# An FFT convolution with an MLP behind it: loads of the first pairs re-ordered, fronts one block earlier, operands moved

## The chip, the cores and the metric

The kernel runs on one core of one Trainium2 chip. Its engines are TensorE (PE, with its weight loads shown apart as PEld), VectorE (DVE), ScalarE (ACT), GpSimd (POOL) and SyncE (SP), which here does nothing but issue DMAs. The metric is device time in microseconds (us) of one execution; the lower the better.

## The reference

Two batches of 12480 positions and 128 channels are convolved along the positions with a long filter, which a small MLP makes from pos_emb; the result is multiplied by x, and its 24960 rows go through a second MLP (128 to 2048 to 128) with a leaky ReLU.

```python
B, S, D = x.shape                                  # 2, 12480, 128
h_mlp = np.maximum(pos_emb @ w1, 0.0) @ w2
h_filt = h_mlp * np.exp(-0.01 * pos)[:, None]
u = x * v
y = irfft(rfft(u, 2 * S) * rfft(h_filt, 2 * S), 2 * S)[:, :S, :]
h = (x * y).reshape(B * S, D) @ w_in               # w_in 128 x 2048
out = np.maximum(0.01 * h, h) @ w_out              # w_out 2048 x 128
```

## The kernel before

The transforms are written as matrix products of lengths 98 (NA) and 128 (NB). **Stage a** (to about 200 us) transforms batch 0 and the filter along 98. **Stage b** (about 200 to 352 us) goes through 25 chunks of 4 frequency rows, in the order ORD: it makes the filter's spectrum (hp, from es, copied by ScalarE at L710; the result hs is also stored to hspec by DMAs that ScalarE issues at L759), transforms the other axis, multiplies, transforms back into dp, copies dp to ct (back_evac, L205) and stores ct in the scratch array scr2. For the first tile of the next stage the last two chunks don't go through scr2: last_c (L588) moves four rows straight from ct into the tile's buffer cin. The preparation of the MLP's weights runs between the chunks.

**The main loop** takes the rest. Its input is cut into 64 tiles t of 390 rows, 32 (NT) for each batch. For each tile:
- load_tile issues 13 DMAs on SP: load_gx the factors gt (L545) and the rows of x called xm (L551, L553, L556), load_c the transform's rows cin (L576, L579, L582). cin has two buffers, as have gt and xm.
- join (join_hi, join_lo) forms sums and differences of cin: two into cp (L600), two into cq (L609), four more into cp (L611). They run on POOL, for tile 0 on VectorE (join_lo alone). cp has one buffer.
- front, first half: 16 matmuls yp (L822) and the product zt (L825, VectorE). Second half, three blocks later: four transposes zp (L830), three copies zf (L833, L835, ScalarE), the rounded part zh (L841, ScalarE) and the remainder zl (L842, POOL).

The MLP works on pieces k of up to 512 columns; a piece takes up one or two tiles. For each of 16 blocks f of the hidden layer m1 issues three matmuls (L849, L850, L851: zh and zl against the high and low parts of the weights), ScalarE and VectorE apply the activation into rh and rl, and three blocks later m2 adds three more matmuls into acc (L881, L882, L883). So a block is six matmuls on PE. When a piece is complete, finish copies its columns out (ot, L896), and at block 4 of the next piece, for a second tile at block 8, transposes them (op, L905, copied by ScalarE to os, L907) and stores them. yp, zp and op are allocated under one PSUM tag, io, with one buffer. The convolution of batch 1 (conv) is fed in between the blocks until about 1090 us.

Everything around the blocks is placed by a table of slots i = 16 k + f. ends[t] is the slot of the second half of front(t): three slots before the piece that first reads the tile, and at least 8 before the next tile's. The first half stands at ends[t] - 3, the join at ends[t] - 11, the loads at ends[t - 2] + 1.

```python
e = min(e - 8, first[t] * NF - 3)
ends[t] = e
...
at(ends[t] - (11 if t % NT > 1 else 8), "join", t)
at(ends[t] - 3, "front", t)
at(ends[t], "front", t)
```

The matmuls of the MLP's m1 and m2 read their moving operands zh, zl, rh and rl from SBUF; in the built program these tiles start 32 bytes past a multiple of 64. Those of the conv (th, tl, ph, pl, L137) start at a multiple of 64.

Of the kernel before, what the change touches and what calls it, by code (L numbers as in the profile page):

```python
# [8 lines left out]
F32 = mybir.dt.float32  # L9
# [21 lines left out]
def tile_conv_mlp(ctx, tc, x, v, pos_emb, w1, w2, w_in, w_out, cf, cr, cg, cb, ci, cw, out):  # L31
    nc = tc.nc
    B, S, D = x.shape
    FO = pos_emb.shape[1]
    DFF = w_in.shape[1]
    NF = DFF // 128
    ROWS = S // NB
    NCH = (NA + KC - 1) // KC
    R0 = 96
    L, H = slice(0, HB), slice(HB, 2 * HB)  # L40
    MID = KH // KC
    ORD = [*range(MID + 1, NCH), MID, *range(MID)]
# [9 lines left out]
    scr2 = [dram.tile([NA, 2 * HB * 256 + 1088], F32, name=f"scr2_{b}")[:, :2 * HB * 256].rearrange(  # L52
        "k (r m e) -> k r m e", r=2, m=HB) for b in range(B)]
# [56 lines left out]
    def run(g):  # L110
        for _ in g:
            pass
# [86 lines left out]
        eng.dma_start(out=scr2[b][k0:k0 + n].rearrange("k r m e -> (r m) k e"),  # L199
                          in_=ct[:, :n].rearrange("p k s d -> p k (s d)"))  # L200

    def back_evac(dp, ct, n):

        for s in range(2):
            nc.scalar.copy(ct[:, :n, s, :], dp[s][:, :n * D].rearrange("p (k d) -> p k d", d=D))  # L205
            yield


    with tc.manual_schedule():
# [3 lines left out]
        def fetch_a(c):  # L213
            ft = s0.tile([128, MC1 * 4 * NA], F32, tag="s0", name="ft1", bufs=3)[:NA].rearrange(
                "a (m p e) -> a m p e", m=MC1, p=2)
            nc.sync.dma_start(out=ft, in_=cf[:, c * MC1:(c + 1) * MC1])
            xv = []
            for i, src in enumerate((x, v)):
                t = s0.tile([128, 1024], F32, tag=f"s{1 + i}", name="xv1", bufs=3 - i)[:NA, :2 * MC1 * D].rearrange(
                    "a (p m d) -> a p m d", p=2, d=D)  # L220
                load_tokens(t, src[1], c * MC1, MC1)
                xv.append(t)
            got[c] = ft, xv
# [312 lines left out]
        xring = Ring("xm", [128, 2, 2, D], slice(32, 64), slice(96, 128))  # L536
        gring = Ring("gt", [128, 4 * NA + 32], (slice(None), slice(4 * NA, None)))
        NT = HB // 2
        ld, z, acc = {}, {}, {}

        def load_gx(t):
            b, mp = divmod(t, NT)
            g = gring()
            for r in range(2):
                nc.sync.dma_start(out=g[KH * r:KH * r + KH, :4 * NA],  # L545
                                  in_=cg[:KH, mp, r].rearrange("k p m a -> k (p m a)"))
            xt = xring()
            ms = slice(2 * mp, 2 * mp + 2)
            full = x[b, :(NA - 2) * NB, :].rearrange("(i w p n) d -> w i p n d", w=2, p=2, n=HB)
            for w in range(2):  # L550
                nc.sync.dma_start(out=xt[64 * w:64 * w + KH - 1], in_=full[w, :, :, ms, :])  # L551
            r0 = (NA - 2) * NB
            nc.sync.dma_start(out=xt[KH - 1:KH],  # L553
                              in_=x[b, r0:r0 + NB, :].rearrange("(o p n) d -> o p n d", o=1, p=2)[:, :, ms, :])
            r0 += NB + 2 * mp
            nc.sync.dma_start(out=xt[GAP - 1:GAP, 0], in_=x[b, None, r0:r0 + 2, :])  # L556
            ld[t] = (None, g, xt)

        def load_c(t):
            b, mp = divmod(t, NT)  # L560
            ci_t = mlp.tile([NA, 3, 2, 2, D], F32, tag="cin", name="cin")
            ld[t] = (ci_t, *ld[t][1:])
            rows_c(t, 1, 0, KH)
            if t:
                rows_c(t, 0, 0, KH)
            else:
                rows_c(t, 0, MID * KC, KH)

        def rows_c(t, j, lo, hi):

            b, mp = divmod(t, NT)
            ci_t = ld[t][0]
            ms = slice(2 * mp, 2 * mp + 2)
            ks = slice(KH * j + lo, KH * j + hi)
            for r in range(2):
                nc.sync.dma_start(out=ci_t[KH * r + lo:KH * r + hi, j].rearrange("k m s d -> k (m s d)"),  # L576
                                  in_=scr2[b][ks, r, ms, :].rearrange("k m e -> k (m e)"))
            if j:
                nc.sync.dma_start(out=ci_t[KH + lo:KH + hi, 2].rearrange("k m s d -> k (m s d)"),  # L579
                                  in_=scr2[b][ks, 0, ms, :].rearrange("k m e -> k (m e)"))  # L580
                for i in range(2):
                    nc.sync.dma_start(out=ci_t[lo:hi, 2, :, i, :], in_=scr2[b][ks, 1, ms, D - D * i:2 * D - D * i])  # L582

        def last_c(ct, k0, n):

            for r in range(2):
                for m in range(2):
                    nc.sync.dma_start(out=ld[0][0][KH * r + k0:KH * r + k0 + n, 0, m],  # L588
                                      in_=ct[HB * r + m:HB * r + m + 1, :n])

        def load_tile(t):
            load_gx(t)
            load_c(t)

        def join_hi(t):

            ci_t, g, xt = ld[t]
            cp = mlp.tile([NA, 2, 2, 2, D], F32, tag="cp", name="cp", bufs=1)
            for p, op in ((0, ALU.add), (1, ALU.subtract)):
                nc.gpsimd.tensor_tensor(out=cp[:, p, 1], in0=ci_t[:, 1 + p, :, 0, :], in1=ci_t[:, 1 + p, :, 1, :], op=op)  # L600
            ld[t] = ci_t, g, xt, cp

        def join_lo(t):
# [10 lines left out]
        with ExitStack() as st:  # L614
# [81 lines left out]
            def ahead(n):  # L696
                for _ in range(4 * n):
                    next(conv)
# [13 lines left out]
            def evac(c):  # L712
                ct = sbb.tile([128, KC, 2, D], F32, tag="ct", name="ct", bufs=2)
                k0, n = chunk(c)
                run(back_evac(dps.pop(c), ct, n))
                if c in ORD[-2:]:
                    last_c(ct, k0, n)
                store_back(0, c, ct, nc.scalar)

            eh, dps = {}, {}  # L720
            ahead(A0)
            next(conv)
            hidden(ORD[0])
            for i, c in enumerate(ORD):
                if i + 2 < NCH:
                    load_b(ORD[i + 2])
                if i == NCH - 9:
                    load_gx(0)
                    load_c(0)
                if i == NCH - 5:  # L730
                    join_hi(0)
                if i == NCH - 3:
                    load_gx(1)
                if i == NCH - 1:
                    rows_c(0, 0, 0, (MID - 2) * KC)
                if i in FETCH:
                    fetch_a(1 + FETCH.index(i))
                if i == NCH - 2:
# [4 lines left out]
                n = chunk(c)[1]  # L743
# [40 lines left out]
            load_c(1)  # L784
            mult_a(2)
            ahead(A2)
            fetch_a(3)
            run(wprep)
            ahead(A3)

# [25 lines left out]
        def front(t):  # L816
# [3 lines left out]
            for q in range(4):  # L820
                for w in range(2):
                    nc.tensor.matmul(yp[64 * w:64 * w + 64, q, :], g[:NA, NA * q + w:NA * q + w + 127:2],  # L822
                                     cp[:, q // 2, w, q % 2, :], start=True, stop=True)
            zt = sm.tile([128, 4, D], F32, tag="zt", name="zt", bufs=1)
            nc.vector.tensor_tensor(out=zt[:GAP], in0=yp[:GAP], in1=xt[:GAP].rearrange("a p m d -> a (p m) d"),  # L825
                                    op=ALU.mult)
            yield
# [90 lines left out]
        first = [next(pieces_of(t))[0] for t in range(total)]  # L918
        ends, e = {}, NTL * NF
        for t in reversed(range(1, total)):  # L920
            e = min(e - 8, first[t] * NF - 3)
            ends[t] = e
        steps = {}

# [140 lines left out]
```

## Time and profile before

| what | value |
|---|---|
| runs | 1757.57 us median of 3 (1754.39 to 1758.05) |
| profiled execution | 1754.5 us |
| its span | 1752.7 us |
| busy, PE | 1666.5 us (95% of the span) |
| busy, DVE | 1112.9 us (63%) |
| busy, ACT | 984.4 us (56%) |
| busy, POOL | 828.7 us (47%) |
| mean granted TensorE clock | 0.977 |

The span is the time between the first and the last instruction of the profiled execution; the execution's own time holds 1.8 us more. A granted clock of 1.00 is TensorE's upper level (2.4 GHz), 0.50 its lower (1.2 GHz); a stretch's value in between is a mean over both. Matmuls overlap: their durations are longer than the distance of their starts, so what one costs in a stream is read from the starts.

### The profile page before, as it was taken

The numbers are of one execution on the slowest core, as the hardware profiler recorded it, in microseconds if no ns is written. First come the engines' busy times: TensorE is split into PE (matmuls) and PEld (weight loads), VectorE is DVE, ScalarE is ACT, GpSimd is POOL, SyncE is SP. The second block draws the span as 40 slices with busy tenths as digits, with TensorE's granted clock in tenths as the row PEclk, the third lists the DMA queues.
The fourth block names the chain that finished last, engine by engine and source line by source line (L and its number), as shares of the span: only waits on it lengthen the run. The fifth ranks groups of instructions, "written<-read, shape, count | busy, mean of one in ns | idle before, by whom it ended". The sixth has DMA issues, their size and how long they took to land. (4 is left out here: it accounts for less than half of the span.)

```text
span 1752.7 us, 27421 instructions
## 1 busy us (share of the span) xinstructions
PE 1666.5 (95%) x9185; PEld 1331.7 (76%) x9185; DVE 1112.9 (63%) x1702; ACT 984.4 (56%) x2006; POOL 828.7 (47%) x860
## 2 busy tenths in 40 slices
PE   6787899869999999999999999999999999999998
PEld 6687455468888878777877787877777777887778
DVE  4576688735545565555655554477777777777775
ACT  2222354424444466666767665566666666666666
POOL 3453121234434367777767674443544454345330
PEclk9889999979999999999999999999999999999999
DMA  9898999864667475656656551312212121212110
GB/s 234 240 269 243 296 324 321 283 180 142 182 172 195 117 197 164 176 149 175 167 144 181 159 153 49 96 49 64 70 49 77 42 73 53 66 46 71 58 32 19
DMA packets 166680, 253.27 MB, mean 145 GB/s; under 512 B 14623, under 2 KB 119347, under 8 KB 163467
## 3 DMA queue, kind: packets, MB, share of 16 engines
q1 hardware_dynamic: 146394, 225.82, 45.2%
q10 hardware_dynamic: 20144, 25.69, 4.3%
q8 instruction: 73, 1.20, 0.3%
q14 instruction: 69, 0.56, 0.1%
HBM read 167.95 MB, written 83.43 MB: 143 GB/s over the span
## 5 line engine op out<-in xcount | busy, mean ns | idle before, releaser
L856 DVE SCALAR_TENSOR_TENSOR rl<-mh,rh 128x512 fp32r<-128x512 f32 (+2 forms) x400 | 269.3, 676 | 315.9 <-ACT rh L855 312.9
L866 DVE TENSOR_TENSOR rl<-r,rh 128x512 fp32r<-128x512 f32 (+1 forms) x400 | 326.2, 828 | 124.6 <-ACT rh L865 117.5
L855 ACT ACTIVATE rh<-mh 128x512 fp32r<-128x512 f32 (+2 forms) x400 | 234.6, 589 | 216.6 <-PE mh L851 199.7
L861 ACT ACTIVATE r<-mh 128x512 f32<-128x512 f32 (+1 forms) x400 | 235.0, 588 | 178.1 <-PE mh L851 165.2
L849 PE MATMUL mh<-zh,w_in_h 128*128 128x512 f32 (+3 forms) x800 | 330.4, 413 | 2.1 <-ACT zh L841 1.3
L850 PE MATMUL mh<-zl,w_in_h 128*128 128x512 f32 (+3 forms) x800 | 313.7, 392 | 6.4 <-POOL zl L842 6.2
L851 PE MATMUL mh<-zh,w_in_l 128*128 128x512 f32 (+3 forms) x800 | 312.6, 391 | 0.0
L883 PE MATMUL acc<-rh,w_out_l 128*128 128x512 f32 (+3 forms) x800 | 312.3, 390 | 0.0
L881 PE MATMUL acc<-rh,w_out_h 128*128 128x512 f32 (+3 forms) x800 | 312.1, 390 | 0.0
L882 PE MATMUL acc<-rl,w_out_h 128*128 128x512 f32 (+3 forms) x800 | 312.1, 390 | 0.0
L611 POOL TENSOR_TENSOR cp<-cq,cp 98x256 f32<-98x256 f32 x252 | 218.6, 867 | 19.8
L842 POOL TENSOR_TENSOR zl<-zf,zh 128x390 fp32r<-128x390 f32 (+24 forms) x110 | 72.3, 670 | 317.1 <-ACT zh L841 194.0
L600 POOL TENSOR_TENSOR cp<-cin 98x256 f32<-98x256 f32 x128 | 103.4, 828 | 202.7 <-PE yp L822 122.9
L849 PEld LDWEIGHTS mh<-zh,w_in_h 128*128 128x128 f32 x800 | 151.1, 189 | 37.6 <-issue 7.6
L850 PEld LDWEIGHTS mh<-zl,w_in_h 128*128 128x128 f32 x800 | 151.7, 190 | 34.9 <-POOL zl L842 10.0
L882 PEld LDWEIGHTS acc<-rl,w_out_h 128*128 128x128 f32 x800 | 150.8, 188 | 34.0 <-DVE rl L866 0.6
L881 PEld LDWEIGHTS acc<-rh,w_out_h 128*128 128x128 f32 x800 | 150.9, 189 | 33.4
L883 PEld LDWEIGHTS acc<-rh,w_out_l 128*128 128x128 f32 x800 | 150.7, 188 | 33.3
L851 PEld LDWEIGHTS mh<-zh,w_in_l 128*128 128x128 f32 x800 | 151.0, 189 | 32.5
L863 DVE CAST rh<-r 128x512 fp32r<-128x512 f32 (+1 forms) x200 | 126.7, 634 | 28.6 <-ACT r L861 25.3
L865 ACT CAST rh<-r 128x512 fp32r<-128x512 f32 (+1 forms) x200 | 121.9, 610 | 6.4
L609 POOL TENSOR_TENSOR cq<-cin 98x256 f32<-98x256 f32 x126 | 104.7, 831 | 2.1 <-DMA cin<-scr 2.1
(152 smaller groups left out, 2369.4 us busy)
## 6 DMA issues: line engine op xcount, KB each, us to landing
cin<-scr SPq DMA_DIRECT2D x318, 98.0 KB
hd<-hspec SPq DMA_DIRECT2D x48, 512.0 KB
scr<-o SPq DMA_DIRECT2D x32, 588.0 KB
bin<-scr SPq DMA_DIRECT2D x23, 768.0 KB
scr1b<-o SPq DMA_DIRECT2D x32, 392.0 KB
hspec<-hs ACTq DMA_DIRECT2D x48, 256.0 KB
scr<-ct ACTq DMA_DIRECT2D x24, 512.0 KB
xm<-in_x_dram SPq DMA_DIRECT2D x128, 96.0 KB
```

Of the source, the lines that this page charges most:

```text
L611: eng.tensor_tensor(out=cp[:, p, w], in0=cq[:, p], in1=cp[:, p, 1], op=op)
L849: nc.tensor.matmul(hp, w_in_h[:, fs], zh, start=True, stop=False)
L850: nc.tensor.matmul(hp, w_in_h[:, fs], zl, start=False, stop=False)
L851: nc.tensor.matmul(hp, w_in_l[:, fs], zh, start=False, stop=True)
L855: nc.scalar.activation(out=rh, in_=hp, func=AF.Relu)
L856: nc.vector.scalar_tensor_tensor(out=rl, in0=hp, scalar=0.0, in1=rh, op0=ALU.max, op1=ALU.subtract)
L861: nc.scalar.activation(out=r, in_=hp, func=AF.Lrelu, alpha=0.01)
L863: nc.vector.tensor_copy(rh, r)
L866: nc.vector.tensor_tensor(out=rl, in0=r, in1=rh, op=ALU.subtract)
L881: nc.tensor.matmul(ap, w_out_h[:, f, :], rh, start=(f == 0 and at0[k] >= S), stop=False)
L882: nc.tensor.matmul(ap, w_out_h[:, f, :], rl, start=False, stop=False)
L883: nc.tensor.matmul(ap, w_out_l[:, f, :], rh, start=False, stop=(f == NF - 1))
```

## The change

The loads of cin's upper halves (one DMA of r = 0, one of r = 1, and so on) become a generator, upper_c, and for tile 0 one of its five steps is taken per chunk from the 16th chunk on, where before all thirteen DMAs of tile 0 stood at the 17th. gt and xm of tile 0 move to the second last chunk, those of tile 1 behind the last rows of tile 0. The two sums of join_hi for tile 0 move from POOL to VectorE, directly ahead of its join_lo. Of the last chunk's four DMAs from ct to cin two are issued by ScalarE, and VectorE makes the second of the two copies to ct. load_tile issues cin ahead of gt and xm. Tile 2 is loaded behind the first half of front(0), and the fetch fetch_a(3) for batch 1, which stood ahead of it, follows. The ends of the fronts are 4 slots ahead of the piece in place of 3; the joins and loads, which count from them, move along. zt is allocated with 856 numbers per partition in place of 512; the tiles behind it, zh, zl, rh and rl among them, then start at a multiple of 64 bytes in the built program, and those of the conv 32 bytes past one.

```diff
-    def back_evac(dp, ct, n):
+    def back_evac(dp, ct, n, other=None):
         for s in range(2):
-            nc.scalar.copy(ct[:, :n, s, :], dp[s][:, :n * D].rearrange("p (k d) -> p k d", d=D))
+            (s and other or nc.scalar.copy)(ct[:, :n, s, :], dp[s][:, :n * D].rearrange("p (k d) -> p k d", d=D))
...
+        def upper_c(t):
+            cin[t] = mlp.tile([NA, 3, 2, 2, D], F32, tag="cin", name="cin")
+            b, ms = t // NT, slice(2 * (t % NT), 2 * (t % NT) + 2)
+            ks = slice(KH, 2 * KH)
+            for r, j in ((0, 1), (1, 1), (0, 2)):
+                p0 = KH * (r if j == 1 else 1)
+                nc.sync.dma_start(out=cin[t][p0:p0 + KH, j].rearrange("k m s d -> k (m s d)"),
+                                  in_=scr2[b][ks, r, ms, :].rearrange("k m e -> k (m e)"))
+                yield
...
-        def last_c(ct, k0, n):
+        def last_c(ct, k0, n, engs):
             for r in range(2):
                 for m in range(2):
-                    nc.sync.dma_start(out=ld[0][0][KH * r + k0:KH * r + k0 + n, 0, m],
+                    engs[m].dma_start(out=cin[0][KH * r + k0:KH * r + k0 + n, 0, m],
                                       in_=ct[HB * r + m:HB * r + m + 1, :n])
         def load_tile(t):
+            load_c(t)
             load_gx(t)
-            load_c(t)
         def join_hi(t):
...
+            eng = nc.gpsimd if t else nc.vector
...
-                if i == NCH - 9:
+                if NCH - 10 <= i < NCH - 5:
+                    next(first_c)
+                if i == NCH - 2:
                     load_gx(0)
-                    load_c(0)
-                if i == NCH - 5:
-                    join_hi(0)
-                if i == NCH - 3:
-                    load_gx(1)
                 if i == NCH - 1:
                     rows_c(0, 0, 0, (MID - 2) * KC)
+                    load_gx(1)
...
-            fetch_a(3)
...
-            zt = sm.tile([128, 4, D], F32, tag="zt", name="zt", bufs=1)
+            zt = sm.tile([128, 856], F32, tag="zt", name="zt", bufs=1)[:, :4 * D].rearrange("a (q d) -> a q d", d=D)
...
-            e = min(e - 8, first[t] * NF - 3)
+            e = min(e - 8, first[t] * NF - 4)
...
         frt = front(0)
+        join_hi(0)
         join_lo(0)
         next(frt)
+        load_tile(2)
+        fetch_a(3)
```

How the change moves rows on the engines is shown at two places. The first is SP's queue between the loads of tile 1 and those of tile 2. In before two fetches for batch 1 (the second ends in the first rows here, L73 and L75) and a store of the conv (L421) stand ahead of tile 2's loads (gt, xm, cin_3247):

```order
L75 DMA xv1_3199<-in_x_dram 1x2x512
L73 DMA xv1_3203<-in_v_dram 96x2x512
L73 DMA xv1_3203<-in_v_dram 1x2x512
L75 DMA xv1_3203<-in_v_dram 1x2x512
L421 DMA scr1b_61<-o1_3106 98x4x256 x2
L545 DMA gt_1329<-in_cg_dram 49x392 x2
L551 DMA xm_1323<-in_x_dram 48x2x256 x2
L553 DMA xm_1323<-in_x_dram 1x2x256
L556 DMA xm_1323<-in_x_dram 1x256
L576 DMA cin_3247<-scr2_0_63 49x512 x2
L579 DMA cin_3247<-scr2_0_63 49x512
L582 DMA cin_3247<-scr2_0_63 49x2x128 x2
```

After the change tile 2's loads (cin_3173, gt, xm) stand directly behind the last loads of tile 1 (cin_3118), and the first fetch (L216, L73) behind them:

```order
L586 DMA cin_3118<-scr2_0_63 49x512 x2
L565 DMA cin_3173<-scr2_0_63 49x512 x3
L569 DMA cin_3173<-scr2_0_63 49x2x128 x2
L586 DMA cin_3173<-scr2_0_63 49x512 x2
L545 DMA gt_1329<-in_cg_dram 49x392 x2
L551 DMA xm_1323<-in_x_dram 48x2x256 x2
L553 DMA xm_1323<-in_x_dram 1x2x256
L556 DMA xm_1323<-in_x_dram 1x256
L216 DMA ft1_3187<-in_cf_dram 98x1568
L73 DMA xv1_3189<-in_x_dram 96x2x512
L73 DMA xv1_3189<-in_x_dram 1x2x512
L75 DMA xv1_3189<-in_x_dram 1x2x512
```

So thirteen loads have moved ahead of two fetches and a store, and cin stands ahead of gt and xm. The second place is PE, in a piece where two tiles become due. In before the transposes op stand at the end of one block and zp at the end of the next; in brackets stands whose semaphore a row waits for:

```order
L905 MATMUL op<-ident,ot 98x128 [waits DVE_49]
L905 MATMUL op<-ident,ot 98x128 [waits Activation_49]
L905 MATMUL op<-ident,ot 98x128 x2
L849 MATMUL mh<-zh,w_in_h 128x512
L850 MATMUL mh<-zl,w_in_h 128x512
L851 MATMUL mh<-zh,w_in_l 128x512
L881 MATMUL acc<-rh,w_out_h 128x512
L882 MATMUL acc<-rl,w_out_h 128x512
L883 MATMUL acc<-rh,w_out_l 128x512
L830 MATMUL zp<-ident,zt 128x113 [waits Activation_49]
L830 MATMUL zp<-ident,zt 128x113 x3
```

After the change, in the same piece (L836 is the line of zp now, L911 that of op, L855 that of the first m1 matmul, L887 to L889 those of m2):

```order
L887 MATMUL acc<-rh,w_out_h 128x512 [waits Activation_49]
L888 MATMUL acc<-rl,w_out_h 128x512
L889 MATMUL acc<-rh,w_out_l 128x512
L836 MATMUL zp<-ident,zt 128x113 [waits DVE_49]
L836 MATMUL zp<-ident,zt 128x113 x3
L911 MATMUL op<-ident,ot 98x128 [waits PE_49,Activation_49]
L911 MATMUL op<-ident,ot 98x128 x3
L855 MATMUL mh<-zh,w_in_h 128x512 [waits DVE_49]
```

zp has moved up by a block and stands directly ahead of op, which takes the same PSUM buffer: op waits for ScalarE, whose last copy out of zp sets it free. PE's rows have zp directly ahead of op 15 times now, nowhere before.

## Rows read from the trace of the kernel before

**Rows 1.** The page's part 1: engine, busy us, share of the span, instructions.

```profile
PE 1666.5 (95%) x9185; PEld 1331.7 (76%) x9185; DVE 1112.9 (63%) x1702; ACT 984.4 (56%) x2006; POOL 828.7 (47%) x860
```

**Rows 2.** Waits of PE up to 390 us: waited for, us in all, times, longest.

```profile
PE hp L749 <- ACT es L710: 10.6, 5, 3.6
...
PE yp L822 <- POOL cp L611: 5.0, 2, 4.6
```

**Rows 3.** Waits of PE from 390 us on.

```profile
PE mh L850 <- POOL zl L842: 6.2, 8, 1.0
PE yp L822 <- POOL cp L611: 2.0, 4, 0.8
```

**Rows 4.** Timeline around the second seam: start, us, engine, line, idle time and releaser.

```profile
369.76 1.98 PE L822 MATMUL yp<-cp,gt 98*64 98x128 f32 x16
...
374.55 0.74 SPq L545 DMA_DIRECT2D gt<-in_cg_dram  x2
...
380.62 0.74 POOL L600 TENSOR_TENSOR cp<-cin 98x256 f32<-98x256 f32 x1 [11.41 <-DMA cin<-scr]
...
383.69 0.72 POOL L600 TENSOR_TENSOR cp<-cin 98x256 f32<-98x256 f32 x1 [2.33 <-DMA xm<-in_x_dram]
...
386.46 1.91 PE L822 MATMUL yp<-cp,gt 98*64 98x128 f32 x8 [4.63 <-POOL cp L611]
...
387.97 1.52 POOL L611 TENSOR_TENSOR cp<-cq,cp 98x256 f32<-98x256 f32 x2
...
388.74 1.92 PE L822 MATMUL yp<-cp,gt 98*64 98x128 f32 x8 [0.37 <-POOL cp L611]
```

**Rows 5.** Timelines of PE and POOL around one zl wait.

```profile
1169.23 1.10 PE L822 MATMUL yp<-cp,gt 98*64 98x128 f32 x16
...
1177.53 0.40 PE L883 MATMUL acc<-rh,w_out_l 128*128 128x512 f32 x1
1177.76 0.40 PE L849 MATMUL mh<-zh,w_in_h 128*128 128x512 f32 x1
1177.78 1.73 POOL L842 TENSOR_TENSOR zl<-zf,zh 128x366 fp32r<-128x366 f32 x2
1179.19 0.50 PE L850 MATMUL mh<-zl,w_in_h 128*128 128x512 f32 x1 [1.03 <-POOL zl L842]
```

**Rows 6.** Stretches: us, busy (x instructions) by engine, granted clock, DMA share, GB/s.

```profile
345.00:350.00 5.00, 5.00 (x40) 3.98 (x39) 4.24 (x8) 2.42 (x5) 0.00 (x0) 1.00 0.59 200
...
385.00:390.00 5.00, 2.94 (x14) 1.75 (x15) 0.00 (x0) 0.00 (x0) 4.69 (x7) 0.62 0.39 121
390.00:395.00 5.00, 5.00 (x25) 4.63 (x22) 1.82 (x3) 1.36 (x3) 2.78 (x2) 0.70 0.31 85
```

**Rows 7.** Timelines of PE and ScalarE around the zp of the same tile.

```profile
1174.57 0.55 PE L830 MATMUL zp<-ident,zt 113*128 113x113 f32 x4
1174.89 0.48 PE L849 MATMUL mh<-zh,w_in_h 128*128 128x512 f32 x1
1175.48 0.36 ACT L835 COPY zf<-zp 128x196 f32<-128x196 f32 x1
1175.87 0.61 ACT L841 CAST zh<-zf 128x366 fp32r<-128x366 f32 x2
```

**Rows 8.** Timeline of the first seam.

```profile
351.92 4.67 SPq L588 DMA_DIRECT2D cin<-ct  x4
...
357.92 0.43 DVE L609 TENSOR_TENSOR cq<-cin 98x256 f32<-98x256 f32 x1 [3.63 <-DMA cin<-ct]
...
358.90 2.36 PE L822 MATMUL yp<-cp,gt 98*64 98x128 f32 x14 [6.56 <-issue]
```

**Rows 9.** PE's lines by form, 410 to 1740 us: busy, mean ns.

```profile
L883 PE MATMUL acc<-rh,w_out_l 128*128 128x512 f32 x734 | 290.4, 396 | 0.0
...
L137 PE MATMUL cv<-th,mb_l 128*128 128x512 f32 x48 | 19.0, 396 | 0.0
...
L137 PE MATMUL cv<-ph,mi_h 128*128 128x512 f32 x46 | 18.0, 392 | 0.0
```

More of the change, by code (lines that the diff above doesn't have):

```diff
@@ L538, in tile_conv_mlp @@
         NT = HB // 2
-        ld, z, acc = {}, {}, {}
+        ld, cin, z, acc = {}, {}, {}, {}
         def load_gx(t):
@@ L556, in load_gx @@
             nc.sync.dma_start(out=xt[GAP - 1:GAP, 0], in_=x[b, None, r0:r0 + 2, :])
-            ld[t] = (None, g, xt)
-        def load_c(t):
[L560 to L567, printed above, removed]
+            ld[t] = (g, xt)
+        def upper_c(t):
[7 more added lines that the diff above has]
+                yield
+            for i in range(2):
+                nc.sync.dma_start(out=cin[t][:KH, 2, :, i, :], in_=scr2[b][ks, 1, ms, D - D * i:2 * D - D * i])
+            yield
+            if t == 0:
+                rows_c(t, 0, MID * KC, KH)
+                yield
+        def load_c(t):
+            run(upper_c(t))
+            rows_c(t, 0, 0, KH)
         def rows_c(t, j, lo, hi):
             b, mp = divmod(t, NT)
-            ci_t = ld[t][0]
+            ci_t = cin[t]
             ms = slice(2 * mp, 2 * mp + 2)
@@ L577, in rows_c @@
                                   in_=scr2[b][ks, r, ms, :].rearrange("k m e -> k (m e)"))
[L578 to L582, printed above, removed]
-        def last_c(ct, k0, n):
+        def last_c(ct, k0, n, engs):
             for r in range(2):
                 for m in range(2):
-                    nc.sync.dma_start(out=ld[0][0][KH * r + k0:KH * r + k0 + n, 0, m],
+                    engs[m].dma_start(out=cin[0][KH * r + k0:KH * r + k0 + n, 0, m],
                                       in_=ct[HB * r + m:HB * r + m + 1, :n])
         def load_tile(t):
+            load_c(t)
             load_gx(t)
-            load_c(t)
         def join_hi(t):
-            ci_t, g, xt = ld[t]
+            ci_t = cin.pop(t)
+            g, xt = ld[t]
+            eng = nc.gpsimd if t else nc.vector
             cp = mlp.tile([NA, 2, 2, 2, D], F32, tag="cp", name="cp", bufs=1)
             for p, op in ((0, ALU.add), (1, ALU.subtract)):
-                nc.gpsimd.tensor_tensor(out=cp[:, p, 1], in0=ci_t[:, 1 + p, :, 0, :], in1=ci_t[:, 1 + p, :, 1, :], op=op)
+                eng.tensor_tensor(out=cp[:, p, 1], in0=ci_t[:, 1 + p, :, 0, :], in1=ci_t[:, 1 + p, :, 1, :], op=op)
             ld[t] = ci_t, g, xt, cp
@@ L714, in evac @@
                 k0, n = chunk(c)
-                run(back_evac(dps.pop(c), ct, n))
+                end = c == ORD[-1]
+                run(back_evac(dps.pop(c), ct, n, nc.vector.tensor_copy if end else None))
                 if c in ORD[-2:]:
-                    last_c(ct, k0, n)
+                    last_c(ct, k0, n, (nc.sync, nc.scalar if end else nc.sync))
                 store_back(0, c, ct, nc.scalar)
             eh, dps = {}, {}
+            first_c = upper_c(0)
             ahead(A0)
```

## The prediction

> **What bounds the kernel now.** I read the page first. TensorE (PE) is busy 1666.5 of 1752.7 us, 95%, the next engine, VectorE, 63% [rows 1]. So time can be won where PE stands still, where its clock falls, or where each matmul gets shorter; work that moves between the other engines counts only if PE waits for it. The waits of PE, read before and after 390 us, show what it stands still for in the places the diff touches: 10.6 us in stage b for ScalarE's copy of the filter spectrum (es), and 5.0 us for POOL, whose sums cp feed the yp matmuls [rows 2]; later 6.2 us in eight waits for POOL's zl, and 2.0 us in four more for cp [rows 3].
>
> **Second seam, tile 2 (381 to 393 us): -8.9.** PE reaches the yp matmuls of tile 2 and waits 4.63 us for POOL's sums [rows 4]. POOL began them at 380.62, after 11.41 us of idling for tile 2's loads of cin. SP issued the first of tile 2's loads (gt) only at 374.55, behind a store and two fetches for batch 1, and cin's later still. The sixteen yp matmuls then take 1.91 + 0.37 + 1.92 = 4.2 us, against 1.10 us for a group of sixteen later on [rows 5]: 3.1 us lost. The granted clock is 0.62 and 0.70 in the two stretches from 385 to 395 us [rows 6], which is TensorE's lower level (1.2 GHz) from 386.5 to about 393 us, after PE's idling. From 390.7 to 393 us the blocks behind yp thus lose half of 2.3 us, 1.2. Together 4.6 + 3.1 + 1.2 = 8.9 us.
>
> The change issues tile 2's thirteen loads before both fetches, as SP's order shows. In before POOL had all of cin within 383.69 - 374.55 = 9.1 us of the first issue [rows 4]. Now the first issue comes behind tile 1's loads, when VectorE has read the cin buffer that tile 2 takes: its last sums of tile 0 end some 2 us behind the start of yp at 358.90 [rows 8], at about 361. By 370 the data is there. One cp buffer exists; yp of tile 1 has read it at 369.76 + 1.98 = 371.7. POOL then needs 0.74 for its first sum and at most 5.8 (383.69 to 387.97 + 1.52) for the others, so cp is complete at about 378.2. PE went idle at 386.46 - 4.63 = 381.8 and comes a block of 1.07 us sooner now (the 1.40 us worked out below, for 390 columns in place of 512), at 380.8. Slack 2.6 us, so the whole wait goes, and with it the fall of the clock. What is late next: zl of tile 1 stands behind these sums on POOL as it did, and the two fetches are wanted by conv work some ten blocks on. If the loads land later than about 374 us the wait returns piece by piece, up to the full 8.9.
>
> **Fronts one block ahead: -7.5.** Each of the eight zl waits looks alike [rows 5]: yp at 1169.23, behind it POOL's sums of the next tile, only behind them zl at 1177.78. PE's matmuls start 0.23 us apart (L883 at 1177.53, L849 at 1177.76), so L850 was due at 1177.99; it starts at 1179.19: 1.03 us of waiting by the row, 1.20 us by the starts. So each costs its wait and 0.17: 6.2 + 8 x 0.17 = 7.5 us. A block of six matmuls of 0.233 us lasts 1.40 us. With yp, zp and the sums one block earlier, zl is there 1.40 us sooner against the piece that reads it, over the largest loss of 1.20: all eight go. The four waits of 0.8 us and less for cp (the place near 1120 us, where batch 1 begins) move with their own sums and with the zl ahead of them; I take nothing, and bound it at -4 us (2.0 of waiting and a lowered clock behind it), since load_tile now loads cin ahead of the other parts there.
>
> **The same edit's price: +14.3.** finish transposes the output (op, L905) in block 4 of a piece; yp, zp and op share one PSUM buffer ("io"). In before zp stood in block 5 of those pieces where two tiles begin, so a block of matmuls lay between op and zp and hid the copies out of the buffer. With -4 in place of -3, zp lands in block 4, directly ahead of op. PE's order has that 15 times, and op then waits for ScalarE's three copies zf<-zp. What it costs stands in any zp of before [rows 7]: zp starts at 1174.57, PE would go on at 1174.89, the last copy starts at 1175.48 and lasts 0.36, so the buffer is free at 1175.84: 0.95 us, 15 x 0.95 = 14.3 us. From below: no reason excludes that some are shorter, but this distance depends on ScalarE alone, which is free when zp comes in nearly all of the 64; 0.8 each gives 12. From above: with the 0.17 of the zl waits 1.12 each, 16.8. I take 0.95. This eats all that the move wins, which is where I differ from what the edit seems to offer.
>
> **First seam (350 to 362 us): -1.3.** Of the last chunk four small DMAs go from ct into cin; SP needs 4.67 us to issue them, VectorE's cq waits 3.63 us for the data until 357.92, yp starts at 358.90 [rows 8]. Now two stay on SP, two go to ScalarE's queue, and VectorE makes the second copy. Bounds: half of the issuing, -2.3, and 0, since conv work of both engines and the two sums of join_hi (2 x 0.43, as cq) now stand ahead of cq on VectorE. I take -1.3. The Trainium skill, "DMA: Bandwidth & Descriptors", Issuing engines are not separate DMA queues, says that issuing from several engines only saves the sequencer's time, usually small beside the transfer; by that this term is near 0 and the sum 1.3 higher. The row of 4.67 us for four issues speaks for more.
>
> **Stage b: -1.0.** The burst of thirteen loads at one chunk is spread to one per chunk, tile 1's part moves behind the last chunk's rows. PE halts there for es, five times, the longest 3.6 us [rows 2], where ScalarE is held up by issuing its hspec stores. The bytes stay; some 350 KB move behind the last chunk's loads, where the DMA engines are 0.59 busy at 200 GB/s [rows 6]; at 200 / 0.59 = 340 GB/s they are worth 1.0 us of a full queue. Bounds 0 and -3.6 (one halt gone). I take -1.0. POOL's two early sums, which stood in idle time, cost nothing by going.
>
> **Operand addresses: -3.5.** Padding zt by 1,376 bytes moves zh, zl, rh and rl in the built program from 32 bytes past a multiple of 64 to a multiple of 64. A 512-column matmul on them lasts 396 ns; in the conv, on ph, which starts at a multiple of 64, 392, but on th, which does too, 396 [rows 9]. So between 0 and 4 ns for six lines of 734, 4,400 matmuls: 0 to -18 us. The rows contradict each other; I take 0.8 ns, -3.5 us, nearer to nothing.
> The Trainium skill, "Advanced Engine Details and Errata", SBUF Cachelines, gives lines of 16 bytes and a penalty only where each access takes another one. Both starts are multiples of 16; by that this term is 0. No run here shows more.
>
> **Sum.** -8.9 - 7.5 + 14.3 - 1.3 - 1.0 - 3.5 = -7.9 us. Against the profiled execution's 1754.5 that is 1746.6. The median of the runs shown is 3.1 above the profiled execution; the middle of those four times (1754.39, 1754.5, 1757.57, 1758.05) is 1.5 above it, so I say **1748.1**. About 3.5 us (0.2%) is what a measurement tells from nothing.
>
> **Rivals.**
> - *Addresses count more, or the start of batch 1 gains too* (-4 ns, or 2 ns and -4 us): 6 to 14 us below the forecast, about 1740. For: ph's 392 ns. Against: th's 396. 0.15.
> - *Addresses do nothing*: 1748.1 + 3.5 = 1751.6. For: th. Against: ph. 0.18.
> - *Tile 2's loads don't come in time*, so that the change doesn't do there what it says: 1748.1 + 8.9 = 1757. For: they meet batch 1's fetches, and SP waits for two buffers on the way. Against: 2.6 us of slack. 0.08.
> - *The collisions cost double* (slower): op behind zp delays not PE alone. On ScalarE zh (0.61 [rows 7]) and the copy os of op, taken as long, then stand ahead of the activation of the block, and if PE's next block waits for that, each collision costs 0.95 + 1.2 = 2.15 us, 32 in all: 1748.1 + 18 = 1766. By the sum it turns slower by 0.2% above 0.95 + (7.9 + 3.5) / 15 = 1.7 us each. Against: three mh buffers and three blocks of distance to the second matmuls. 0.10.
> - *Forecast*, 1743 to 1751: 0.49.
>
> Faster by over 0.2%: 0.49 + 0.15 + most of 0.18 less the forecast's upper edge, 0.78. Within: the rest of these and 0.08, 0.12. Slower: 0.10. The range leaves out the slower rival and the end of the addresses: 1739 to 1757.
>
> **What the profile after would show.** Tile 2: no wait of yp for cp near 381, clock 1.00 from 385 to 395. Main loop: no zl waits; instead 15 waits of op for ScalarE's zf, 0.9 to 1.1 each. The means of L849 to L883 at 394 to 396 ns if the address term holds. First seam: yp some 1 us sooner against the last dp. The prediction fails most likely at the addresses, which no row of before decides, or where a collision draws a second wait behind it.

## The result and the profile after

The changed kernel takes 1734.96 us (median of 4 executions, 1733.7 to 1740.38) against 1755.98 us (4 executions of the kernel before, 1753.04 to 1758.05): ratio 0.9884, 95% interval 0.9862 to 0.9906. That is some 21 us faster; 7.9 were forecast, and the time lies below the range. The profiled execution took 1735.8 us, 18.7 less than that of before.

PE's busy time has fallen by 16 us, though it does the same instructions as before [rows 1]. From the page's part 1 of the changed kernel:

```profile
PE 1650.2 (95%) x9185; PEld 1327.1 (77%) x9185; DVE 1108.7 (64%) x1705; ACT 985.4 (57%) x2005; POOL 833.0 (48%) x858
```

So most of what was won is shorter work of PE, at the seam or in every matmul, and only the smaller part less waiting. The waits of PE up to 390 us: the wait of yp for POOL's cp [rows 2] is gone, that of the first seam ("issue") is left.

```profile
PE hp L756 <- ACT es L717: 7.1, 6, 3.2
PE yp L828 <- issue: 6.3, 1, 6.3
```

From 390 us on the eight zl waits [rows 3] are gone, and 15 waits of op for the copies zf have come:

```profile
PE op L911 <- ACT zf L841: 11.4, 15, 0.8
PE yp L828 <- POOL cp L618: 1.2, 2, 0.8
```

At the second seam [rows 4] the timeline of the changed kernel has SP issuing tile 2's cin from 359.12 us on, POOL's sums from 370.93 to 377.01, and yp of tile 2 at 380.55 without a wait:

```profile
359.12 0.95 SPq L565 DMA_DIRECT2D cin<-scr  x3
...
365.97 0.42 SPq L556 DMA_DIRECT2D xm<-in_x_dram  x1
...
370.93 1.43 POOL L607 TENSOR_TENSOR cp<-cin 98x256 f32<-98x256 f32 x2 [3.51 <-PE yp L828]
...
375.45 1.56 POOL L618 TENSOR_TENSOR cp<-cq,cp 98x256 f32<-98x256 f32 x2
...
380.55 1.10 PE L828 MATMUL yp<-cp,gt 98*64 98x128 f32 x16
```

The granted clock (the third number from the end in these stretches) stays at 1.00 where it was 0.62 and 0.70 [rows 6]:

```profile
385.00:390.00 5.00, 5.00 (x32) 4.85 (x31) 2.26 (x4) 3.14 (x10) 3.53 (x6) 1.00 0.43 130
390.00:395.00 5.00, 5.00 (x33) 4.56 (x32) 2.67 (x5) 2.38 (x6) 4.77 (x6) 1.00 0.33 109
```

One of the 15 collisions (op directly behind zp in their one buffer), in the timelines of PE and ScalarE (to be read beside [rows 7]): op starts at 1103.89, behind the end of the third copy, 1103.83; by the distance zp to the next row in [rows 7], 0.32 us, it was due at 1102.89. That is 1.00 us by the starts, for a wait of 0.77 by the row.

```profile
1102.57 0.55 PE L836 MATMUL zp<-ident,zt 113*128 113x113 f32 x4
1103.48 0.35 ACT L841 COPY zf<-zp 128x196 f32<-128x196 f32 x1
1103.89 0.64 PE L911 MATMUL op<-ident,ot 128*98 128x128 f32 x4 [0.77 <-ACT zf L841]
1104.57 0.59 ACT L913 COPY os<-op 98x512 f32<-98x512 f32 x1 [0.18 <-PE op L911]
```

At the first seam [rows 8] ScalarE and SP share the four issues. VectorE no longer idles directly ahead of cq, where join_hi's two sums stand now. It idles 4.03 us ahead of a sum of the conv (o) instead, for ScalarE's copy a1s, and that copy starts only when ScalarE's three issues are done, at 352.92 + 1.40 = 354.32:

```profile
351.03 1.85 ACTq L593 DMA_DIRECT2D cin<-ct  x2
351.99 2.34 SPq L593 DMA_DIRECT2D cin<-ct  x2
352.92 1.40 ACTq L199 DMA_DIRECT2D scr<-ct  x1
354.36 0.59 ACT L104 COPY a1s<-hp 98x512 f32<-98x512 f32 x1 [4.11 <-DMA cin<-ct]
...
354.98 0.69 DVE L106 TENSOR_TENSOR o<-hp,a1s 98x512 f32<-98x512 f32 x1 [4.03 <-ACT a1s L104]
...
356.85 0.42 DVE L616 TENSOR_TENSOR cq<-cin 98x256 f32<-98x256 f32 x1
...
357.83 2.57 PE L828 MATMUL yp<-cp,gt 98*64 98x128 f32 x15 [6.28 <-issue]
```

And the MLP's matmuls are shorter [rows 9], by some 3 ns in the mean, while those of the conv on ph, which have moved the other way, are longer (lines by form, 410 to 1720 us):

```profile
L889 PE MATMUL acc<-rh,w_out_l 128*128 128x512 f32 x729 | 286.6, 393 | 0.0
...
L888 PE MATMUL acc<-rl,w_out_h 128*128 128x512 f32 x729 | 284.8, 391 | 0.0
...
L137 PE MATMUL cv<-ph,mi_h 128*128 128x512 f32 x46 | 18.4, 400 | 0.0
```

Matmuls overlap, so the cost is the distance of the starts. Over all pairs of neighbouring 512-column matmuls of the MLP whose starts lie 215 to 260 ns apart (some 3,900 in each trace) the mean is 233.2 ns before and 229.9 ns after. The conv's three lines on ph and pl go the other way by the starts too: 229.2, 232.4 and 230.9 ns before, 232.7, 235.6 and 233.5 after.

### The profile page after: what moved, and what is told of

It is laid out like the page before. It is cut to its first block, busy times and chain, and to the rows that moved or that the text cites. A ratio compares the mean times of both kernels' runs of the same rounds, so it can differ in the third digit from the quotient of the medians.

```text
span 1734.0 us, 27418 instructions
## 1 busy us (share of the span) xinstructions
PE 1650.2 (95%) x9185; PEld 1327.1 (77%) x9185; DVE 1108.7 (64%) x1705; ACT 985.4 (57%) x2005; POOL 833.0 (48%) x858
## 4 chain that ended last, share of the span: by engine, by line
PE 78%; DMA 9%; DVE 5%; issue 3%; SPq 2%; ACT 2%; POOL 1%; ACTq 0%; POOLq 0%; DVEq 0%
PE mh L855 11%; PE mh L857 10%; PE mh L856 10%; PE acc L889 10%; PE acc L887 10%; PE acc L888 10%; PE cv L137 4%; PE yp L828 4%; PE cv L408 3%; DMA ft<-in_cf_dram 2%; DMA xt<-in_x_dram 2%; PE op L911 2%; DMA scr<-o 1%; PE zp L836 1%; DMA scr<-ct 1%
## 5 line engine op out<-in xcount | busy, mean ns | idle before, releaser
L855 PE MATMUL mh<-zh,w_in_h 128*128 128x512 f32 (+3 forms) x800 | 329.8, 412 | 1.9 <-ACT zh L847 1.3
L887 PE MATMUL acc<-rh,w_out_h 128*128 128x512 f32 (+3 forms) x800 | 310.3, 388 | 0.0
L856 PE MATMUL mh<-zl,w_in_h 128*128 128x512 f32 (+3 forms) x800 | 310.0, 388 | 0.0
L889 PE MATMUL acc<-rh,w_out_l 128*128 128x512 f32 (+3 forms) x800 | 310.0, 388 | 0.0
L888 PE MATMUL acc<-rl,w_out_h 128*128 128x512 f32 (+3 forms) x800 | 308.3, 385 | 0.0
L618 POOL TENSOR_TENSOR cp<-cq,cp 98x256 f32<-98x256 f32 x252 | 212.4, 843 | 19.8
L855 PEld LDWEIGHTS mh<-zh,w_in_h 128*128 128x128 f32 x800 | 151.1, 189 | 37.0 <-issue 9.9
L889 PEld LDWEIGHTS acc<-rh,w_out_l 128*128 128x128 f32 x800 | 150.3, 188 | 31.5
L887 PEld LDWEIGHTS acc<-rh,w_out_h 128*128 128x128 f32 x800 | 150.4, 188 | 30.4
L869 DVE CAST rh<-r 128x512 fp32r<-128x512 f32 (+1 forms) x200 | 114.3, 572 | 38.4 <-ACT r L867 35.8
L616 POOL TENSOR_TENSOR cq<-cin 98x256 f32<-98x256 f32 x126 | 113.3, 899 | 1.0 <-DMA cin<-scr 1.0
```

Of the source, the lines that this page charges most:

```text
L618: eng.tensor_tensor(out=cp[:, p, w], in0=cq[:, p], in1=cp[:, p, 1], op=op)
L855: nc.tensor.matmul(hp, w_in_h[:, fs], zh, start=True, stop=False)
L856: nc.tensor.matmul(hp, w_in_h[:, fs], zl, start=False, stop=False)
L887: nc.tensor.matmul(ap, w_out_h[:, f, :], rh, start=(f == 0 and at0[k] >= S), stop=False)
L888: nc.tensor.matmul(ap, w_out_h[:, f, :], rl, start=False, stop=False)
L889: nc.tensor.matmul(ap, w_out_l[:, f, :], rh, start=False, stop=(f == NF - 1))
```

## Experiments

Beside the times a table worked out from the starts of the matmuls in each trace is used: how long the program takes from one of its points to the next. "Piece 0" is from its first m1 matmul to that of piece 1; piece 24 is the one around the start of batch 1. Stage a, which no kernel here changes, is counted to the first matmul of stage b (ep) in the table; it takes 171 to 177 us in these profiles, so a difference of a microsecond or two ahead of the seam can't be read from one profile; from piece 1 on, kernels with the same main loop agree to some 0.2 us in a piece. Piece 0 holds the end of the lower clock behind the first seam, which lasts differently long: with the same loads of tile 2 it takes 21.16 us in e1 and 23.91 in e4, at a mean granted clock of 0.92 and 0.80.

| us | before | after | e1 | e2 | e3 | e4 | e7 | e8 |
|---|---|---|---|---|---|---|---|---|
| stage b to last dp | 175.0 | 172.5 | 173.9 | 177.0 | 174.2 | 172.6 | 177.0 | 174.6 |
| last dp to first yp | 9.06 | 8.79 | 8.05 | 8.93 | 7.89 | 7.88 | 8.09 | 8.91 |
| piece 0 | 30.29 | 22.22 | 21.16 | 30.47 | 21.67 | 23.91 | 29.53 | 23.88 |
| pieces 1 to end, without 24 | 1331.1 | 1323.4 | 1335.1 | 1320.0 | 1319.9 | 1309.9 | 1323.2 | 1309.8 |
| piece 24 | 24.07 | 22.12 | 22.14 | 25.34 | 24.05 | 19.31 | 22.12 | 19.31 |

**e1 and e2: the addresses.** e1 is the changed kernel with zt unpadded, e2 the kernel before with zt padded and nothing else (the same two lines the other way round). The tiles behind zt all move along.

```diff
-            zt = sm.tile([128, 856], F32, tag="zt", name="zt", bufs=1)[:, :4 * D].rearrange("a (q d) -> a q d", d=D)
+            zt = sm.tile([128, 4, D], F32, tag="zt", name="zt", bufs=1)
```

> The changed kernel with zt back at 512 numbers, so that zh, zl, rh and rl start 32 bytes past a multiple of 64 again. Theory (operand addresses carry most of the gain that the sum missed: in the trace of the changed kernel these matmuls start 229.9 ns apart, before 233.2; 3.3 ns x some 4,490 = 15 us): 15 us slower than the changed kernel, about 1750 us, ratio to the kernel before 0.996, starts 233 ns apart. Rival (the addresses do nothing, the shorter distance comes with the order of the fronts): as the changed kernel, 1735 us, ratio 0.988, starts 230 ns apart.

> The kernel before with zt padded to 856 numbers and nothing else. Theory (addresses): 15 us faster than before, about 1741 us, ratio 0.9915, starts 230 ns apart; zl waits and the wait of tile 2 as before. Rival (addresses do nothing alone): ratio 1.000, starts 233 ns apart.

e1: 1743.34 us, ratio to before 0.9922 (0.9903 to 0.994), starts 233.2 ns apart. e2: 1746.64 us, ratio 0.9932 (0.9916 to 0.9947), starts 230.0 ns apart. The distance goes with the padding alone, whatever the order of the fronts. It isn't the other engines' work beside the matmuls either: in pairs with VectorE, ScalarE and GpSimd busy all the while it is 233.2 ns before and 229.5 after (some 460 pairs each), with ScalarE alone 233.0 and 228.9 (some 300 each). The price is smaller than the 15 us expected: in the loop without piece 24 the pad is worth 1335.1 - 1323.4 = 11.7 us in the changed kernel and 1331.1 - 1320.0 = 11.1 us in the kernel before. Two rows of each timeline show it by eye; here nine steps of e1 take 2.11 us, 234 ns each:

```profile
1300.54 0.40 PE L857 MATMUL mh<-zh,w_in_l 128*128 128x512 f32 x1
...
1302.65 0.40 PE L889 MATMUL acc<-rh,w_out_l 128*128 128x512 f32 x1
```

and eleven steps of the changed kernel 2.52 us, 229 ns each:

```profile
1309.84 0.39 PE L855 MATMUL mh<-zh,w_in_h 128*128 128x512 f32 x1
...
1312.36 0.39 PE L889 MATMUL acc<-rh,w_out_l 128*128 128x512 f32 x1
```

**e3 and e4: the fronts.** e3 puts the fronts back to 3 slots in the changed kernel; e4 keeps the 4 and lets two fronts of one piece stand 7 slots apart, so that zp falls into the block behind op.

```diff
-            e = min(e - 8, first[t] * NF - 4)
+            e = min(e - 8, first[t] * NF - 3)      # e3
+            e = min(e - 7, first[t] * NF - 4)      # e4
```

> The changed kernel with the fronts 3 slots ahead again. Theory (in the changed kernel op behind zp costs PE 0.76 us by the waits and up to 0.95 by the starts in 15 places, 11.4 to 14 us, and the zl waits it removed were worth 7.5): the 15 waits of op for zf go, the eight zl waits come back, 4 to 6.5 us faster than the changed kernel, about 1730 us. Rival (the collisions are paid back elsewhere, only the zl waits count): 7.5 us slower, 1742 us.

> The changed kernel with a distance of 7 slots in place of 8 between the fronts of two tiles that begin in one piece, so that zp falls in the block behind op again, and the other tiles keep their 4 slots. Theory: neither waits of op for zf nor of L856 for zl, 11 to 14 us faster than the changed kernel, about 1722 us, ratio to before 0.981. Rival (seven slots are too few: POOL's sums, 7.3 us and more, and zl come late for the next tile): new waits of yp for cp or of L856 for zl, 1730 us or more.

e3: 1731.42 us, ratio 0.9849 (0.9829 to 0.9868). e4: 1716.15 us, ratio 0.9768 (0.9747 to 0.9788), the fastest kernel of this study. In e3 the collisions are gone and the zl waits back:

```profile
PE mh L856 <- POOL zl L848: 6.8, 8, 1.1
PE yp L828 <- POOL cp L618: 2.1, 4, 0.8
```

In e4 neither is left, and no new wait of their size stands in their place. It gains more than the 11 to 14 us expected, 13.5 in the loop without piece 24 and 2.8 in piece 24:

```profile
PE mh L855 <- DVE rl L862: 0.7, 1, 0.7
PE op L911 <- ACT ot L902: 0.5, 1, 0.5
PE yp L828 <- POOL usp L496: 0.3, 1, 0.3
```

In the loop without piece 24 the collisions cost 1323.4 - 1309.9 = 13.5 us. 14 of the 15 stand there (the one shown above is in piece 24), so 0.96 each. The starts say much the same: from zp to op it takes 1.32 us in the mean of the 15, from zp to the next matmul in the other 49 places 0.32, so 1.00 each and 14.9 in all. Getting the zl waits out is worth 1319.9 - 1309.9 = 10.0 us: 8.7 in the eight pieces that have such a wait in e3, 1.4 in other pieces, all ahead of piece 24, where the conv is fed in. In the same loop fronts at 4 with the old spacing lose 3.5 us against fronts at 3 (1323.4 - 1319.9), as e1 against before without the pad does (1335.1 - 1331.1 = 4.0). Piece 24 gives 2 us of that back: 24.05 against 22.12.

**e5, e6 and e9: where the operands stand, buffer by buffer.** The theory behind e5 and e6 was that a start at a multiple of 64 bytes is what counts. All three have e4's fronts; they make the tiles of rh and rl longer, so that their five buffers start at different places (528, 516 and 552 numbers; e9 also has a gap of 56 numbers between rh and rl, and zt at 600).

```diff
-            rh = sm.tile([128, WIDE], F32R, tag="rh", name="rh", bufs=DEEP + 2)[:, :w]
-            rl = sm.tile([128, WIDE], F32R, tag="rl", name="rl", bufs=DEEP + 2)[:, :w]
+            rh = sm.tile([128, 528], F32R, tag="rh", name="rh", bufs=DEEP + 2)[:, :w]
+            rl = sm.tile([128, 528], F32R, tag="rl", name="rl", bufs=DEEP + 2)[:, :w]
```

> The kernel with spacing 7, and the five buffers each of rh and rl 2112 bytes apart in place of 2048, so that each starts another 64 bytes further on (rh at 192 to 448, rl at 512 to 768 past a multiple of 2048), all at multiples of 64. Theory (what counts is a start at a multiple of 64): matmuls on all ten buffers start 230 ns apart, the time is that of spacing 7 within 2 us (1716). Rival (192 past a multiple of 2048, or equal places of all operands, is what counts): the buffers differ among each other by 2 ns and more, some back at 233; up to 1723 us.

> The kernel with spacing 7, and the buffers of rh and rl 2080 bytes apart, so that they start at a multiple of 64 and 32 bytes past one by turns (rh: 0, 32, 0, 32, 0; rl: 32, 0, 32, 0, 32). Theory (a start at a multiple of 64): the second matmuls on the buffers at 0 start some 230 ns apart or less, on those at 32 some 233; half of the 4,400 matmuls (those of rh and rl) lose 3.3 ns in half of the cases, 3.6 us slower than spacing 7, 1720 us. Rival (the place against the other operands counts, not 64): no difference between the two sorts of buffers.

> The kernel with spacing 7, zt padded to 600 numbers and the five buffers each of rh and rl 2208 bytes apart, so that buffer n of rh and buffer n of rl start at the same place modulo 512: 192, 352, 0, 160 and 320 for n = 0 to 4 (zh and zl at 192; before, all four stand at 352; a gap of 224 bytes between rh and rl, filled once by VectorE). Theory (the place modulo 512 sets the distance of the starts): within this one run the second matmuls of blocks with buffer 1 (352) start 233 ns apart, those with buffer 0 (192) 228 to 231, as in the changed kernel, and m1's on zh and zl 229 to 231. Rival (the place modulo 2048, or the place of one operand against the next, sets it): buffer 0 and buffer 1 don't differ so; m1's starts, with zh and zl at 1216 modulo 2048 in place of 192, change. The whole: 1716 to 1724 us.

e5: 1722.23 us, ratio 0.9803 (0.9778 to 0.9829). e6: 1724.28 us, 0.982 (0.979 to 0.9849). e9: 1719.18 us, 0.9795 (0.9768 to 0.9821). Mean distance from the start of one of m2's matmuls to that of the next, in ns, for buffers 0 to 4 (their starts modulo 512 ahead of it):

```text
e5  rh 192 256 320 384 448   rl 0 64 128 192 256
    rh,w_out_h  231.4 231.3 234.2 229.4 230.8
    rl,w_out_h  231.3 231.0 230.3 229.9 233.9
    rh,w_out_l  228.2 228.6 228.5 233.0 234.0
e6  rh 192 224 256 288 320   rl 352 384 416 448 480
    rh,w_out_h  230.2 230.8 233.6 231.7 231.3
    rl,w_out_h  232.2 231.6 232.0 235.1 229.0
    rh,w_out_l  232.9 232.0 233.9 231.3 234.5
e9  rh and rl 192 352 0 160 320
    rh,w_out_h  230.3 231.3 231.6 231.8 232.1
    rl,w_out_h  229.2 229.7 228.2 233.3 231.7
    rh,w_out_l  228.8 234.0 230.9 230.4 233.7
```

Multiples of 64 fall apart as much as the others (e5: 228.2 to 234.2, all of them multiples of 64; e6: buffer 2 of rh, a multiple of 64, is slower than buffer 1 beside it, which is not). That theory has fallen. In e9 the buffers at 192 are the best over the three rows, 229.4 in the mean, and those at 352, the place of before, slower, 231.7; but 352 is not 233 in all three rows. zl, at 192 modulo 512 as in the changed kernel, has 231.7 in e9 and 233.1 in e5 where the changed kernel has 229.5. And behind zh with w_in_h, with zh at 192 in every block, the mean in e9 runs from 228.9 to 236.2 ns when the blocks are counted off by fives, as the buffers of rh and rl go round. So what a matmul takes hangs on more than its own operand's place.

**e10 and e11: all operands at one place.** Two more lengths of zt in e4, 600 and 552 numbers, put all four operands at 192 modulo 512 again (1216 modulo 2048) and at 0 modulo 512.

```diff
-            zt = sm.tile([128, 856], F32, tag="zt", name="zt", bufs=1)[:, :4 * D].rearrange("a (q d) -> a q d", d=D)
+            zt = sm.tile([128, 600], F32, tag="zt", name="zt", bufs=1)[:, :4 * D].rearrange("a (q d) -> a q d", d=D)   # e10
+            zt = sm.tile([128, 552], F32, tag="zt", name="zt", bufs=1)[:, :4 * D].rearrange("a (q d) -> a q d", d=D)   # e11
```

> The kernel with spacing 7 and zt at 600 numbers, so that zh, zl, rh and rl all start at 1216 modulo 2048, which is 192 modulo 512 (with 856 numbers: 192 modulo 2048 and modulo 512; before: 864 and 352). Theory (the place modulo 512, against weights that all start at 128 modulo 512, sets the distance of the starts): as spacing 7, starts 230 ns apart, 1716 us. Rival (the place modulo 2048, or against other tiles): starts up to 233 ns apart, 1716 to 1727 us.

> The kernel with spacing 7 and zt at 552 numbers, so that zh, zl, rh and rl all start at 1024 modulo 2048, 0 modulo 512. Theory (any multiple of 64 does): starts 230 ns apart, 1716 us. Rival (192 modulo 512 is better than other places): starts 231 to 234 ns apart, 1719 to 1730 us.

e10: 1716.89 us, ratio 0.9774 (0.9752 to 0.9797), starts 229.9 (first half of the loop) and 230.1 ns (second) apart. e11: 1724.39 us, ratio 0.9812 (0.9792 to 0.9831), 232.4 ns in both. In these four layouts, with all operands at one place, the distance goes with the place modulo 512: 192 gives 230 ns at two places modulo 2048, 0 gives 232.4, 352 gives 233.2, with the weights at 128 modulo 512 throughout. Three places are no rule, and since every tile behind zt moves along, the runs don't tell whose place it is. A multiple of 64 alone brings 0.8 of the 3.3 ns (e11).

**e7: tile 2's loads.** The changed kernel with fetch_a(3) back in its place and tile 2 left to the table.

```diff
             ahead(A2)
+            fetch_a(3)
             run(wprep)
...
         next(frt)
-        load_tile(2)
-        fetch_a(3)
```

> The changed kernel with fetch_a(3) back ahead of the preparation of the weights and tile 2 loaded from the table's first slot, as before. Theory (tile 2's loads alone set the second seam): yp waits 4 to 5 us for cp there, the clock falls to 0.6 to 0.7 behind it, 8 to 9 us slower than the changed kernel, 1743 us. Rival (the fronts, a block earlier, or the earlier first seam already remove part of it): 4 us slower or less, 1739 us.

1741.5 us, ratio 0.9916 (0.9896 to 0.9937), 6.5 us above the changed kernel where 8 to 9 were expected. The wait is back, and the clock falls, in the waits up to 397 us

```profile
PE yp L829 <- POOL cp L618: 4.2, 3, 3.4
```

and in the stretches:

```profile
380.00:385.00 5.00, 1.29 (x8) 0.87 (x8) 0.52 (x1) 0.00 (x0) 3.72 (x6) 0.92 0.49 148
385.00:390.00 5.00, 4.48 (x18) 3.53 (x17) 1.26 (x2) 0.50 (x1) 4.58 (x4) 0.50 0.49 144
```

Piece 0 takes 29.53 us in place of 22.22. So 7.3 of the 8.1 us by which piece 0 became shorter are the order of these loads, within the scatter that the first seam's clock brings in. Without it the picture is clear: piece 0 times its mean granted clock is 19.2 to 19.8 us in the ten kernels that load tile 2 early, 24.1 in e7 and 25.2 in before.

**e8: the last rows.** e4 with ScalarE making both copies of the last chunk and SP issuing all four DMAs.

```diff
-                run(back_evac(dps.pop(c), ct, n, nc.vector.tensor_copy if end else None))
+                run(back_evac(dps.pop(c), ct, n))
                 if c in ORD[-2:]:
-                    last_c(ct, k0, n, (nc.sync, nc.scalar if end else nc.sync))
+                    last_c(ct, k0, n, (nc.sync, nc.sync))
```

> The kernel with spacing 7, in which ScalarE makes both copies of the last chunk and SP issues all four DMAs from ct to cin again. Theory (the split saves half the issuing, less what stands ahead of cq): last dp to first yp 9.1 us in place of 7.9 to 8.8, about 1 us slower than spacing 7, 1717 us. Rival (the sequencer's time is small beside the transfer): no difference.

1720.45 us, ratio 0.9798 (0.9773 to 0.9823), against 0.9768 for e4: the intervals overlap, the whole time doesn't settle it. The stretch does, for the two edits together: from the last dp to the first yp 8.91 us against 7.88. In e8 SP's four issues take 4.44 us, and VectorE waits for the data, which is there 1.63 us behind the last of them:

```profile
348.58 4.44 SPq L593 DMA_DIRECT2D cin<-ct  x4
...
354.65 0.42 DVE L616 TENSOR_TENSOR cq<-cin 98x256 f32<-98x256 f32 x1 [2.80 <-DMA cin<-ct]
```

In e4 the two queues issue beside each other, and cq follows join_hi's sums at once. What bounds the stretch now is ScalarE: its copy a1s stands behind its three issues, and in all ten profiles with the split the first yp starts 3.47 us behind the start of that copy. So issuing on ScalarE isn't free here: of the 2.2 us that two of the four issues take, only 1.0 is won.

```profile
346.76 1.85 ACTq L593 DMA_DIRECT2D cin<-ct  x2
347.05 2.12 SPq L593 DMA_DIRECT2D cin<-ct  x2
348.65 0.50 ACTq L199 DMA_DIRECT2D scr<-ct  x1
349.20 0.59 ACT L104 COPY a1s<-hp 98x512 f32<-98x512 f32 x1 [3.21 <-DMA cin<-ct]
...
351.69 0.42 DVE L616 TENSOR_TENSOR cq<-cin 98x256 f32<-98x256 f32 x1
```

## Why the prediction was wrong

The direction was right, the size not: -7.9 against -18.7 by the profiled executions. The step that failed is "Operand addresses: -3.5", where I took 0.8 ns out of a range of 0 to 4 and 3.3 came. The second is the start of batch 1, taken at nothing. The rival that names both, given 0.15, comes nearest to what happened. Its two conditions put the time 9.3 or 14.1 us below the forecast, at 1739 or 1734 (its "6" doesn't come out of them), so the range all but left it out.

- **Operand addresses.** Forecast -3.5, measured -11.7 (e1) and -11.1 (e2). The rows of before held the bound (0 to 4 ns), and the starts moved by 3.3 ns, near its upper end (the lines' means are 391 to 393 ns, but for the first of m1, where 394 to 396 was foretold). Three things misled. I compared how long the rows last, though matmuls overlap and the cost is in the starts. By the starts the trace of before had all six lines of the conv at 229.2 to 232.4 ns (231.4 in the mean) and all six of the MLP at 232.8 to 233.5: 1.8 ns, or 8 us for 4,400 matmuls. The row of ph that I went by (392 ns) is 400 in e1, where ph has its old place. Then I let ph and th cancel each other because they stand at the same place (448 modulo 512); but e5 and e9 show means 4 to 5 ns apart at one and the same place (e5 at 256: 228.6 to 233.9; e9 at 352: 229.7 to 234.0), so that only a layout as a whole has a price. And the edit looked like one of a multiple of 64, which is worth 0.8 ns in e11. The Trainium skill ("Advanced Engine Details and Errata", SBUF Cachelines) has lines of 16 bytes and a penalty only where each access takes another one. What I worked out from it, no difference between two multiples of 16, didn't hold: 233.2, 232.4 and 229.9 ns at three such places. Why 192 modulo 512 is good stays open.
- **Fronts one block ahead.** The eight zl waits are gone, as said. Forecast -7.5; e3 against e4 gives -10.0. The waits themselves are 6.8 in e3, and the eight pieces that hold them lose 8.7, so 1.9 more hang on them, where 1.4 (0.17 each) were counted. The other 1.4 us lie in pieces without such a wait, while the conv is fed in; what they are was not settled.
- **The collisions.** 15 waits of op for zf, as said; forecast +14.3 at 0.95 each, measured 13.5 for the 14 outside piece 24, 0.96 each, and 1.00 by the starts (the waits alone are 11.4, 0.76 each, less than the 0.9 to 1.1 that the profile was to show). This term held. The rival that they cost double has fallen: in e4, which removes them, 13.5 us come back and not 32.
- **Second seam.** Forecast -8.9, measured -8.1 in piece 0, 7.3 of it by e7; the mechanism held, and the size within what the first seam's clock does to piece 0. POOL's sums ended at 377.01 where 378.2 was worked out, yp came at 380.55 where 380.8 was.
- **First seam.** Forecast -1.3. In nine of ten profiles of kernels with the split the stretch from dp to yp is 7.87 to 8.16 us, in the changed kernel's own 8.79, in the three without it (before, e2, e8) 8.91 to 9.06: some 1 us less mostly, 0.3 in the profile compared. There ScalarE's third issue took 1.40 us (0.50 in e4), and its copy a1s, the sums and yp came later by that. The issuing was not small beside the transfer here: 4.44 us for four issues in e8, with the data there 1.63 us behind the last. The Trainium skill ("DMA: Bandwidth & Descriptors", Issuing engines are not separate DMA queues) says that it usually is; these four small transfers are an exception.
- **Stage b.** Forecast -1.0. Measured -2.5 in this pair of profiles, but kernels with the same stage b differ by 4.5 us (172.5 in the changed kernel, 177.0 in e7). The eleven with the new one take 174.2 us in the mean, the two with the old one 175.0 and 177.0. That fits a gain of one to two microseconds and doesn't show it.
- **The start of batch 1.** Taken as nothing with a bound of -4; piece 24 became 1.95 us shorter, though one of the 15 collisions is in it. Of the four waits of yp for cp two are left, and the clock no longer falls behind them: the granted clock was 0.84 and 0.82 from 1120 to 1130 us in before, a loss of some 1.7 us, and is 1.00 in all of piece 24 now. The front and its sums do not move alike there, as I had said they would. The bound was right, the value not. With spacing 7, without collision and waits, piece 24 is 4.8 us shorter than before.

From piece 1 on the terms add up: -11.4 (the mean of e1 and e2) + 13.5 - 10.0 - 1.95 = -9.9 us against -9.7 measured; the prediction had -7.5 + 14.3 - 3.5 = +3.3. Of these 13 us of difference addresses make 8, piece 24 makes 3 (forecast +0.95 for its collision, measured -1.95), zl 2.5; the other collisions make none. Ahead of piece 1 the forecast was -11.2 and the measurement -9.0 (stage a's +1.7 of scatter in it), which takes 2 us of the miss back and agrees within the scatter.

## What to carry to other kernels

A few nanoseconds in each of 4,400 matmuls can decide a case: 3.3 ns were 11 us here, the largest single gain. So price them by what they cost, the distance of the starts, and not by how long the overlapping rows last. Where rows at one and the same condition scatter by as much as the effect, give the far end of the range a real chance. Where one edit moves work by a step in a table, look for what it lands on: a single PSUM buffer made neighbours of two users, and one slot in another place of the same rule (7 for 8) kept the gain of 10 us without the price of 13.5. Read what a wait is worth from the starts behind it, since it can cost more than its own row (1.00 us for 0.76). And a queue that takes over issues holds back its own engine's next work.

## What the runs showed of the hardware

With the clock at 1.00 the distance of back-to-back 512-column matmuls depended on the layout in SBUF: 229.9 to 230.1 ns with all their moving operands at 192 modulo 512 (two places modulo 2048), 232.4 at 0, 233.2 at 352, the weights standing at 128. With mixed places the means by buffer range from 228.2 to 235.1 ns behind m2's matmuls, and they differ by as much behind operands that stand still (228.9 to 236.2 behind zh in e9). It was the same with other engines busy beside the matmuls and with fewer. In the changed kernel the distance also differs by the operand: 228.0 behind rl, 231.0 behind rh with w_out_h, 230.1 behind rh with w_out_l. Some 11 us of 1755 hung on this. Whose place counts was not separated.

A PSUM buffer shared by zp and op cost PE 1.00 us each time the two stood directly behind each other. Four small DMAs took SP 4.44 us to issue (e8); three issues on ScalarE held back its next copy, and with it the first yp, in all ten profiles that have them.
